# Batch 0's second feature half moved to the end of round two, in a Strassen kernel on one Trainium2 core

## Chip, core and metric

The kernel runs on one core of one Trainium2 chip. The metric is device time of one execution in microseconds (us). Before the change the median of three runs is 705.16 us (704.62 to 705.32). The core's engines are named as in the profile: PE (TensorE, matmuls), PEld (its weight loads), DVE (VectorE), ACT (ScalarE), POOL (GpSimd) and SP (SyncE, which here only issues transfers). All data in the computation are float32.

## The reference

Two blocks follow one another. The first is a cross attention between 512 tokens and 32 states, for 8 batches and 8 heads of width 64:

```python
scores = scale * np.matmul(x, state.transpose(0, 1, 3, 2))      # x (8,8,512,64), state (8,8,32,64)
a = softmax(scores)                                            # over the 32 states
xread = np.matmul(a, state)
a2 = softmax(scale * np.matmul(state, x.transpose(0, 1, 3, 2))) # over the 512 tokens
sread = np.matmul(a2, x)
attn = np.concatenate([xread, sread], axis=2)                  # 512 + 32 rows per batch
```

Its output, with the heads side by side, is a matrix of 8 x 544 = 4352 rows and 512 columns. The second block is a feed-forward layer with 2048 features:

```python
h = x @ w_in                                    # w_in (512, 2048)
g = h * erf(softplus(h))
return g @ w_out                                # w_out (2048, 512)
```

Both weights arrive as float64. The kernel reads them as pairs of 32-bit words and makes float32 from them: two ACT and three DVE instructions for each piece.

## The kernel before, in words

**Tiling.** The 2048 features fall into 16 tiles of 128, four groups of four tiles (g = 0 to 3), and two feature halves (u = 0: groups 0 and 1; u = 1: groups 2 and 3). The 4096 token rows are taken batch by batch, 512 at a time; the 256 state rows of all batches (`sread`) are taken together. For the token rows, `xread @ w_in` is not formed by way of `xread`: the states are multiplied by `w_in` first (`mixed`, L1138; `mixed_part`, L613 for batch 0), which gives "mixed weights" of 256 x 512 for a group, and these are multiplied by the transposed attention weights `aT` (the first product). Softplus, erf and the gating multiply follow, then the product with `w_out` (the second product).

**Three schemes of product.** Plain: batch 0's first product (L624, `first`) and second product (L631, `second`), 128x512 matmuls. One level of Strassen, seven products for eight: every other first product (`first_product`, L1237) and the second products of the first half for batches 1 to 5 (`second_product`, L1321). Two levels, 49 products for 64: the second products of the first half for batches 6 and 7 and of the second half for batches 1 to 7 (`twice_product`, L1508). The sums of blocks that Strassen needs are DVE instructions: `sums_a` (L1288) and `sums_y` for activations, `sums_w` (L429) for one level and `sums_b` (L1383) for two levels of `w_out`, L1490 for two levels of activations.

**Stages.** *Start*: load batch 0 and the weights; attention of batch 0; batch 0 is computed whole, all four groups, while the weights are fetched (1 MB at a time into one of three `raw` buffers, L157) and converted (L167, L169 on ACT, L172 to L174 on DVE). All 16 pieces of `w_in` and `w_out` are converted here. The second half of `w_in` is written to a DRAM scratch (`kept_in`, L745), since its place in `ring` is needed. Attention of batch 1 is fitted in. *Round one*: units u = 0 of batches 1 to 7, one after the other. A unit is the sums over its activations, the mixed weights of the next batch, the attention of the batch after that, its second product, and the next batch's first product with softplus, erf and multiply. From each batch's attention `aT` and its sums are saved to DRAM (`keep_y`). In batch 2 the second half's `w_out` and its sums are saved (`keep_w`), since batches 6 and 7 need the space. *States*: the 256 state rows for both halves (L1676, L1725). *Round two*: units u = 1 of batches 1 to 7; `bring_y` reloads the attention. Their results are added to the rows in DRAM by POOL's accumulating transfers (L1556). The last unit, batch 7, instead reloads its output rows into `ring` tiles and adds to them: each quarter result is copied or added from PSUM (ACT L1518, DVE L1523), summed into a block of 128x512, and joined (L1568); four 256 KB stores (L1572) follow.

**What sets the order.** The start follows a list written out by hand (`order0`), one name per step. From the last 40 steps of it on, each operation is declared by `op(engine, cost, at, go, reads, writes, table, land)`. `emit` takes a table `ORDER` with a fixed order for every engine, plays the operations through with their costs to get begin times, and traces them in that order; `at` is not used there. `in_order` then fixes this order on PE, DVE, ACT and SP. `adopt` hands the dependences of one set of buffer names to another.

Of the kernel before, what the change touches and what calls it, by code (L numbers as in the profile page):

```python
# [9 lines left out]
F32 = mybir.dt.float32  # L10
# [7 lines left out]
def kernel(  # L18
# [21 lines left out]
    P = 128  # L40
# [29 lines left out]
    x_t = {}  # L70


    def load_x(b):
        t = xin.tile([P, NC, H, D], F32, name="x")
        for h in range(H):
            nc.sync.dma_start(out=t[:, :, h, :], in_=x[b, h].rearrange("(c p) d -> p c d", p=P))
        x_t[b] = t
# [4 lines left out]
    def in_order(begun, engines=(nc.tensor, nc.vector, nc.scalar, nc.sync)):  # L82

        last = {}
        for i in nc.cur_bb.bb.instructions[begun:]:
            if i.engine in last:
                tc.add_manual_dep(i, last[i.engine].name, mybir.DependencyInfo(
                    mybir.DependencyClass.NoSync, mybir.DependencyReason.DATA), reason="in_order")
            if i.engine in [e.engine for e in engines]:
                last[i.engine] = i  # L90

    begun = traced()

    xq_t = {}

    def load_xq(b, hs=range(H)):
        if b not in xq_t:
            xq_t[b] = xin.tile([P, NI, S // Ns, Ns], F32, name="xq")  # L100
# [8 lines left out]

    st = const.tile([P, B, P], F32, name="st")  # L110
    away0 = ring[:, 1, 0].rearrange("p k i t -> p (k i t)")
    st0 = away0[:, 512:640].rearrange("p (g d) -> p g d", g=2)
    x0 = xin.tile([P, NC, H, D], F32, name="x").rearrange("p c h d -> p (c h d)").rearrange(
        "p (h c d) -> p h c d", h=H, c=NC)
    x_t[0] = x0.rearrange("p h c d -> p c h d")
    for i in range(NI):
        (nc.scalar, nc.sync)[i % 2].dma_start(
            out=x0[:, 2 * i:2 * i + 2].rearrange("p h c d -> p h (c d)"),
            in_=x[0, 2 * i:2 * i + 2].rearrange("h (p c) d -> p h (c d)", c=NC))
        if i == 1:  # L120
            nc.sync.dma_start(out=st0, in_=state[0].rearrange("(g h) n d -> (h n) g d", g=2))

    def load_st(hs):
        for h in hs:
            i, e = h // 2, h % 2
            nc.sync.dma_start(out=st[Ns * i:Ns * i + Ns, 1:B, D * e:D * e + D],
                              in_=state[1:B, h].rearrange("b n d -> n b d"))


    w_in = const.tile([P, NF // 2, NK, P], F32, name="w_in")  # L130
    away = ring[:, :, 2].rearrange("p u k i t -> p u (k i t)").rearrange(
        "p u (j k f) -> p u j k f", k=NK, f=P)
    of_group = [w_in[:, GF * g:GF * g + GF] for g in range(2)] + [away[:, u] for u in range(2)]
    pieces_in = [of_group[j // 2][:, 2 * (j % 2):2 * (j % 2) + 2] for j in range(NF // 2)]
    kept_in = dram.tile([P, NF // 2, NK * P], F32, name="kept_in")
    w_out = const.tile([P, NF, d_model], F32, name="w_out")

    fetched = []

    def weight(dst, src, parts=1):  # L140

        flat = lambda t: t.rearrange("p a b c -> p (a b c)" if len(t.shape) == 4 else
                                     "p a b -> p (a b)")
        if src.dtype == F32:
            fetched.append(nc.sync.dma_start(out=dst, in_=src))
            return [lambda: None] * 2 * parts, [lambda: None] * 3 * parts  # L150
        raw = act.tile([P, 2 * 2 * d_model], U32, name="raw", bufs=3)
        blocks = [(raw, src)]
        if len(src.shape) == 4:
            blocks = [(raw.rearrange("p (h x) -> p h x", h=2)[:, h], src[:, h]) for h in range(2)]
        for to, part in blocks:
            part = part.bitcast(U32)
            fetched.append(nc.sync.dma_start(  # L157
                out=to.rearrange("p (a b) -> p a b", a=part.shape[1]), in_=part))
        n, m = dst.shape[1] // parts, d_model // parts * 4
        on_act, on_dve = [], []  # L160
        for k in range(parts):
            to, words = dst[:, n * k:n * k + n], raw[:, m * k:m * k + m]
            words = words.rearrange("p (n w) -> p n w", w=2)
            lo, hi, to = words[:, :, 0], words[:, :, 1], flat(to)
            d = to.bitcast(U32)
            on_act += [
                lambda to=to, hi=hi: nc.scalar.activation(out=to, in_=hi.bitcast(F32),  # L167
                                                          func=ACTF.Copy, scale=2.0 ** -112),
                lambda lo=lo: nc.scalar.activation(out=lo, in_=lo, func=ACTF.Copy,  # L169
                                                   scale=2.0 ** -29)]  # L170
            on_dve += [
                lambda d=d: nc.vector.tensor_scalar(d, d, 3, None, op0=ALU.logical_shift_left),  # L172
                lambda on=nc.vector, d=d, lo=lo: on.tensor_tensor(d, d, lo, op=ALU.add),
                lambda d=d, hi=hi: nc.vector.scalar_tensor_tensor(  # L174
                    out=d, in0=hi, scalar=0x80000000, in1=d, op0=ALU.bitwise_and,
                    op1=ALU.bitwise_or)]
        return on_act, on_dve

    gw = GF * P

    def weights_in(j):
        return weight(pieces_in[j], moe_w_in[:, 2 * P * j:2 * P * j + 2 * P].rearrange(
            "(k p) (h f) -> p h k f", p=P, f=P), 2 if j == 0 else 1)

    def weights_out(j):
        return weight(w_out[:, 2 * j:2 * j + 2, :],
                      moe_w_out[2 * P * j:2 * P * j + 2 * P].rearrange("(t p) e -> p t e", p=P))

    leads = [0]
# [4 lines left out]

    def lead(out):

        warm(out, leads[0])
        leads[0] = 0

    sT = const.tile([P, NK, 2, Ns, B // 2], F32, name="sT")  # L200
    st00 = away0[:, 768:1024]
    where = {h: (g, q) for g, hs in enumerate(((0, 2, 1, 3), (5, 7, 4, 6)))
             for q, h in enumerate(hs)}
    aT = {}

    def all_of(jobs):
        for f in jobs:
            f()
# [7 lines left out]
    marks = []  # L216

    def scored(b, xT, pool=ps_at, names=("at", "at")):


        s2 = [pool.tile([P, S], F32, name=name) for name in names]
        for i in reversed(range(NI)):
            for e in range(2):
                r, q = slice(D * e, D * e + D), slice(Ns * i, Ns * i + Ns)
                on_pe = nc.tensor.matmul(out=s2[e][q, :], lhsT=st[r, b, q], rhs=xT[r, i, :],
                                         start=True, stop=True)
        marks.append(on_pe)
        return s2

    def scores(b, xT, *pool):  # L230
        s2 = scored(b, xT, *pool)
        on_pe = marks.pop()
        sc = att.tile([P, 2, S], F32, name="sc")
        for e in range(2):
            last = nc.scalar.copy(sc[:, e], s2[e])
        marks[:] = last, on_pe
        return sc, last

    def largest(sc):
        m2 = small.tile([P, 2], F32, name="m2")  # L240
        for e in range(2):
# [1689 lines left out]
```

## Time and profile before

The profiled execution spans 702.93 us; the median of the runs is 705.16 us.

| what | us |
|---|---|
| median of three runs | 705.16 |
| span of the profiled execution | 702.93 |
| PE busy, in the span | 694.6 |
| DVE busy | 571.8 |
| ACT busy | 469.3 |
| POOL busy | 58.9 |
| first product of batch 0 begins | 19.05 |
| first second product of batch 1 begins (L1321) | 126.46 |
| first product of two levels (L1508) begins | 345.86 |
| last matmul begins | 697.65 |

The profiler records one execution. A float32 matmul appears as two MATMUL records, whose starts are one streaming time apart; each record also holds the time that the data needs to run through the array, so successive records overlap, and prices are best taken from the distance between starts. The same holds for short DVE and ACT instructions, to a smaller extent. "Busy" is the time in which an engine has at least one record open. Stretches of one kind on one engine are merged in the timeline and in the chain ("x24" is 24 records).

### The profile page before, as it was taken

How to read it: one execution, taken by the hardware profiler on the slowest of the kernel's cores; microseconds unless marked ns; L12 is line 12 of the kernel's file. 1: busy time of each engine (PE TensorE's matmuls, PEld its weight loads, DVE VectorE, ACT ScalarE, POOL GpSimd, SP SyncE). 2: the span in 40 equal slices, each digit the busy share in tenths (PEclk: the TensorE clock that was granted, in tenths of full speed). 3: DMA queues.
4: the chain of work that ended last, by engine and by line, in shares of the span. 5: the costliest groups of instructions: out<-in, count | busy, mean ns of one | idle time of the engine just before them, and what ended most of it. 6: DMA issues, size and time to landing. Idle time of an engine off the chain costs nothing.

```text
span 702.9 us, 12986 instructions
## 1 busy us (share of the span) xinstructions
PE 694.6 (99%) x5039; PEld 565.4 (80%) x5039; DVE 571.8 (81%) x930; ACT 469.3 (67%) x812; POOL 58.9 (8%) x54
## 2 busy tenths in 40 slices
PE   8999999999999999999999999999999999999997
PEld 7444346687878778787999998798989898989997
DVE  6997887999979788696969753896979587778997
ACT  5999898949576655838473455846585756666842
POOL 0000000000000000000001000102021221212322
PEclk9999999999999999999999999999999999999999
DMA  8869582845648746352234514405152663435665
GB/s 261 260 194 252 191 192 46 201 86 108 179 85 259 198 81 201 55 173 53 93 98 120 161 58 165 98 31 96 17 98 33 111 75 69 60 42 65 104 94 106
DMA packets 159886, 85.54 MB, mean 122 GB/s; under 512 B 123728, under 2 KB 149328, under 8 KB 159056
## 3 DMA queue, kind: packets, MB, share of 16 engines
q1 hardware_dynamic: 146224, 71.59, 36.5%
q0 software_dynamic: 13056, 12.59, 14.3%
q8 instruction: 40, 0.66, 0.4%
q10 hardware_dynamic: 544, 0.52, 0.2%
q14 instruction: 22, 0.18, 0.1%
HBM read 46.27 MB, written 34.73 MB: 115 GB/s over the span
## 4 chain that ended last, share of the span: by engine, by line
PE 94%; DVE 4%; issue 0%; ACT 0%; DVEq 0%; ACTq 0%
PE o L1508 28%; PE o L1321 17%; PE h L1237 17%; PE o L631 8%; PE at L1237 7%; PE o L1725 3%; PE h L1676 3%; PE h L624 2%; PE at L624 2%; PE h L1138 2%; PE at L1138 2%; PE at L1676 1%; PE at L1100 1%; PE h L997 1%; PE at L613 1%; DVE ring L1568 1%
## 5 line engine op out<-in xcount | busy, mean ns | idle before, releaser
L1249 ACT COPY ring<-h 128x512 f32<-128x512 f32 x112 | 64.7, 586 | 84.3 <-PE h L1237 81.2
L1237 PE MATMUL h<-aT,m 128*128 128x256 f32 x336 | 85.1, 380 | 0.0
L1277 DVE TENSOR_TENSOR ring<-ring 128x1024 f32<-128x1024 f32 (+1 forms) x60 | 68.6, 1146 | 14.0 <-ACT ring L1274 13.4
L1321 PE MATMUL o<-w_out,ring 128*128 128x256 f32 x320 | 77.7, 383 | 0.0
L1321 PEld LDWEIGHTS o<-w_out,ring 128*128 128x128 f32 x320 | 59.6, 190 | 15.9 <-issue 5.9
L1259 ACT ACTIVATE ring<-ring 128x512 f32<-128x512 f32 x112 | 66.7, 631 | 6.6 <-PE o L1321 2.1
L1237 PEld LDWEIGHTS h<-aT,m 128*128 128x128 f32 x336 | 61.8, 190 | 10.4 <-ACT ring L1249 0.8
L1288 DVE TENSOR_TENSOR ring<-ring 128x1024 f32<-128x1024 f32 x56 | 67.8, 1217 | 0.3
L631 PE MATMUL o<-w_out,ring 128*128 128x512 f32 x128 | 59.7, 599 | 0.0
L1508 PE MATMUL o<-w_out,w_in 128*128 128x128 f32 x448 | 59.6, 275 | 0.0
L1274 ACT ACTIVATE ring<-ring 128x1024 f32<-128x1024 f32 (+1 forms) x60 | 59.0, 1004 | 0.2
L1321 PE MATMUL o<-raw,ring 128*128 128x256 f32 x240 | 58.9, 381 | 0.1
L1508 PE MATMUL o<-w_out,ring 128*128 128x128 f32 x432 | 58.8, 276 | 0.0
L1508 PEld LDWEIGHTS o<-w_out,ring 128*128 128x128 f32 x432 | 54.1, 192 | 4.2 <-issue 1.7
L1508 PEld LDWEIGHTS o<-w_out,w_in 128*128 128x128 f32 x448 | 56.0, 192 | 1.7 <-issue 0.8
L1556 POOL DMA_DIRECT2D out_dram<-oo x14 | 17.0, 1213 | 448.5 <-ACT o L1529 360.8
L1321 PEld LDWEIGHTS o<-raw,ring 128*128 128x128 f32 x240 | 45.3, 190 | 9.5 <-issue 2.5
L631 PEld LDWEIGHTS o<-w_out,ring 128*128 128x128 f32 x128 | 23.7, 190 | 27.6 <-issue 26.2
L1508 PE MATMUL o<-raw,ring 128*128 128x128 f32 x324 | 44.7, 276 | 0.0
L1508 PEld LDWEIGHTS o<-raw,ring 128*128 128x128 f32 x324 | 41.3, 192 | 2.4 <-issue 1.7
L1251 DVE TENSOR_TENSOR ring<-ring,at 128x512 f32<-128x512 f32 x28 | 19.1, 684 | 23.5 <-ACT ring L1249 21.8
L1508 PE MATMUL o<-raw,xT 128*128 128x128 f32 x288 | 37.3, 275 | 0.0
(289 smaller groups left out, 1391.5 us busy)
## 6 DMA issues: line engine op xcount, KB each, us to landing
raw<-in_moe_w_in_dram SPq DMA_DIRECT2D x16, 512.0 KB, 4.8
raw<-in_moe_w_out_dram SPq DMA_DIRECT2D x8, 1024.0 KB, 5.3
xq<-in_x_dram SPq DMA_DIRECT2D x112, 64.0 KB, 2.5
x<-in_x_dram SPq DMA_DIRECT2D x56, 128.0 KB, 3.2
out_dram<-oo SPq DMA_DIRECT2D x10, 512.0 KB, 3.7
kept_a<-aT SPq DMA_DIRECT2D x7, 512.0 KB, 3.2
aT<-kept_a SPq DMA_DIRECT2D x7, 512.0 KB, 4.6
out_dram<-oo POOLq DMA_DIRECT2D x14, 256.0 KB, 4.4
```

The source lines that it names most:

```text
L624: nc.tensor.matmul(out=h_t[g, i], lhsT=m_t[0, g][:, e, P * i:P * i + P], rhs=aT[0][:, e], start=start, stop=not start)
L631: nc.tensor.matmul(out=acc[r], lhsT=gT[g][:, i, P * r:P * r + P], rhs=w_out[:, GF * g + i, :], start=(made_of[r] == 1), stop=(made_of[r] = ...
L1138: nc.tensor.matmul(out=bank(names[e])[q, :], lhsT=st[r, b, q], rhs=of_group[2 * u + j][r, :, i, :], start=True, stop=True)
L1237: nc.tensor.matmul(out=out_[:, i], lhsT=x_[:, q:q + P], rhs=y_, start=(start and i == 0), stop=(i == 1), skip_group_check=not start)
L1249: op(ACT, 0.5, t, lambda: nc.scalar.copy(out_(), view(bank(name))), [name], w)
L1259: op(ACT, 0.53, t, lambda: nc.scalar.activation(out=part(splane, k), in_=part(hplane, k), func=ACTF.Softplus), area(hplane, ks=[k], os=[o] ...
L1274: op(ACT, 0.085 + 0.875 * share, at + n, lambda s_=s_: nc.scalar.activation(out=s_, in_=s_, func=ACTF.Erf), [], area(splane, ks=[k], os=os ...
L1277: op(DVE, 0.065 + 1.075 * share, at + n + 1, lambda s_=s_, h_=h_: tt(s_, s_, h_, op=ALU.mult), area(hplane, ks=[k], os=os), area(splane, k ...
L1288: op(DVE, 1.14, at + k, lambda k=k, x_=x_, y_=y_, how=how: tt(get("h", k), get(*x_), get(*y_), op=how), area(v[x_[0]], ks=[x_[1]]) + area( ...
L1321: nc.tensor.matmul(out=view(name)[:, h], lhsT=lhs[:, i, :], rhs=weight_of[n]()[:, u, i, :], start=(start and h == 0 and i == 0), stop=(h = ...
L1508: nc.tensor.matmul(out=out_[:, Q2 * k:Q2 * k + Q2], lhsT=lhs[:, k, i], rhs=rhs[:, i], start=first, stop=(k == len(ns) - 1 and i == 1), ski ...
L1676: nc.tensor.matmul(out=bank(bk)[:, P * i:P * i + P], lhsT=x_[:, i, k], rhs=y_[:, k], start=(start and i == 0 and k == 0), stop=(i == GF - ...
```

## The change

- Batch 0's groups 2 and 3 are left out of the start. Its products over groups 0 and 1 stay plain, and its rows are stored from these alone. Its attention is summed and saved like every other batch's (`sums_y(0)`, `keep_y(0)`), and batch 0 becomes the eighth and last unit of round two, in two levels of Strassen. Batch 7, which was last, is now added to DRAM by POOL like the others.
- The weights of the second half are no longer converted in the start. `stage(n)`, 16 times, fetches one tile of `w_in` or `w_out` into half of a `raw` buffer and converts it during round one; a tile of `w_in` goes from there to `kept_in` (eight saves of 256 KB in place of two of 1 MB). The sums of the second half's `w_out` and `keep_w` move from batch 2 to batch 5.
- `order0`, with `start0`, `groups0`, `weights0` and `next0`, is gone. The start is declared by `op` like the rest (`begin0`, `mixed0`, `first0`, `serf0`, `second0`, `put0`, `fetch_pair`, `convert_pair`), with the transfers as a pipe in `emit` (`pipe`, `FIXED`). `ORDER` is new for all five engines, from the first instruction on, and `in_order` now holds for POOL too. Some copies out of PSUM change engine (`BY_VECTOR` names those on DVE). The two exponentials of batch 0's token weights move ahead of the first softplus.
- In the last unit, the last of the five groups of products (`ns == (3,)`) adds its quarter results from PSUM straight into the output tile (`into`), and the last block is stored in three pieces of 128, 64 and 64 KB.

The core of the diff:

```diff
-    def in_order(begun, engines=(nc.tensor, nc.vector, nc.scalar, nc.sync)):
+    def in_order(begun, engines=(nc.tensor, nc.vector, nc.scalar, nc.sync, nc.gpsimd)):
...
-    STARTS = {PE: 0.0, ACT: 1.3, DVE: 2.5, SP: 0.0, GP: 0.0}
+    STARTS = {PE: 0.78, ACT: 0.74, DVE: 1.0, SP: 0.74, GP: 1.0}
     LAG = {PE: 0.24, ACT: 0.16, DVE: 0.17, SP: 0.2, GP: 0.2}
+    FIXED = 2.1
...
-                    free[e] = begin[n] + cost
-                    end[n] = free[e] + land
+                    end[n] = free[e] = begin[n] + cost
+                    end[n] += land
+                    if pipe:
+                        piped = max(piped, end[n]) + pipe
+                        end[n] = piped + FIXED
...
+    def second0(g, r, i, at):
+
+        def go():
+            made_of[r] += 1
+            nc.tensor.matmul(out=bank("o%d" % r), lhsT=gT[g][:, i, P * r:P * r + P],
+                             rhs=w_out[:, GF * g + i, :], start=(made_of[r] == 1),
+                             stop=(made_of[r] == NF // 2))
+
+        op(PE, 0.86, at, go, gT_of(g, i) + [("Wo", GF * g + i), "oacc%d" % r], [])
...
+            if final is not None and ns == (3,):
+                join_others()
+
+                def into(frm, h, q, t, region=region, of_bank=of_bank):
+                    to = mine(0, 1)[:, h, Q2 * q:Q2 * q + Q2]
+                    op(DVE, 0.2, t, lambda: tt(to, to, region[frm](), op=ALU.add),
+                       [of_bank[frm]], area(final, us=[0], ks=[2 + h], os=[q]))
+
+                copy = add = into
...
-            join(0, 1, R3, at + 22)
-            store(0, 1, at + 22)
...
+        if final is not None:
+            for h, qs in (1, slice(0, 2)), (0, slice(0, 1)), (0, slice(1, 2)):
+                cols = slice(Q2 * qs.start, Q2 * qs.stop)
+                op(SP, 0.4, at + 26, lambda h=h, cols=cols: nc.sync.dma_start(
+                    out=quad(0, 1)[:, h, cols], in_=mine(0, 1)[:, h, cols]),
+                   area(final, us=[0], ks=[2 + h], os=range(qs.start, qs.stop)), [], land=2.2)
...
+    for kind, j, k, at, then in (("i", 0, 0, 2.2, 8.5), ("i", 1, 1, 3.3, 13.4), ("o", 0, 2, 5.2, 16),
+                                 ("o", 1, 0, 16.2, 22), ("i", 2, 1, 22.6, 32), ("i", 3, 2, 26.3, 37),
+                                 ("o", 2, 0, 30.5, 39), ("o", 3, 1, 37.2, 43.5)):
+        fetch_pair(kind, j, k, at)
+        convert_pair(kind, j, k, then)
...
+    def stage(n, at):
+        f, k, e = NF // 2 + n // 2, n % 3, n // 2 % 2
+        if n % 2:
+            fetch_out(f, k, 1, at)
+            convert(("o", f), half(k, 1), w_out[:, f], RAW(k, [1]), [("Wo", f)], at + 5)
+        else:
+            fetch_in(f, k, 1, at)
+            convert(("i", f), half(k, 1), mt(3)[:, e], RAW(k, [1]), [("mS", 1, e)], at + 5)
+            op(SP, 0.45, at + 10, lambda: nc.sync.dma_start(
+                out=kept_in[:, f - NF // 2], in_=mt(3)[:, e]), [("mS", 1, e)],
+               [("kin", f - NF // 2)], land=3.0)
+
+    for n in range(NF):
+        stage(n, BASE + 8 + 8 * n)
...
-                          3 - hplane if u and b == B - 1 else None)
+                          3 - hplane if u and b == 0 else None)
...
-            if b == 2:
-                sums_w(1, base + 20, 1, 2, 4, 3)
-                keep_w(base + 30)
+            if b == TWICE - 1:
+                sums_w(1, base + 5, 1, 2, 4, 3)
+                keep_w(base + 12)
...
-    hq = {b: 2 if b % 2 else 1 for b in range(1, B)}
+    turns = [*range(1, B), 0]
+    hq = {b: 2 if b % 2 else 1 for b in turns}
...
-    for b in range(1, B):
...
+    for n, b in enumerate(turns):
+        nxt = turns[n + 1:n + 2]
...
-        unit(b, 1, base + 34.5 * (b - 1), 0, hq[b], follow, between)
+        unit(b, 1, base + 34.5 * n, 0, hq[b], follow, between)
 
     emit()
-    in_order(begun, [nc.tensor, nc.vector, nc.scalar])
+    in_order(begun)
```

## The prediction

> **What bounds the kernel now.** I read the page's busy shares, then the chain that ended last, then busy time by stage, then single rows for prices.
>
> The busy shares and the chain's shares by engine:
>
> ```profile
> PE 694.6 (99%) x5039; PEld 565.4 (80%) x5039; DVE 571.8 (81%) x930; ACT 469.3 (67%) x812; POOL 58.9 (8%) x54
> ...
> PE 94%; DVE 4%; issue 0%; ACT 0%; DVEq 0%; ACTq 0%
> ```
>
> TensorE is the bound from end to end: it is idle for 8.3 us in all. So a change is worth the matmul time that it removes, less the gaps that it opens. Where gaps could open is read from the stages. The cuts are: first product of batch 0 (19.05), first second-layer product of batch 1 (126.46), batch 6, where twice-Strassen begins (345.86), round two's first unit (463.0), last matmul (698.3).
>
> ```profile
> core 0: us, PE busy (x) PEld busy (x) DVE busy (x) ACT busy (x) POOL busy (x), PEclk, DMA share, GB/s
> 0.00:19.05 19.05, 16.44 (x197) 14.28 (x197) 12.35 (x27) 10.92 (x17) 0.69 (x6) 1.00 0.80 263
> 19.05:126.46 107.41, 107.41 (x565) 50.59 (x564) 91.71 (x128) 99.42 (x126) 0.00 (x0) 1.00 0.69 193
> 126.46:345.86 219.40, 218.39 (x1558) 175.54 (x1557) 189.95 (x324) 144.23 (x241) 0.00 (x0) 1.00 0.55 136
> 345.86:463.00 117.14, 117.14 (x871) 107.74 (x871) 83.38 (x137) 66.15 (x123) 7.38 (x6) 1.00 0.37 105
> 463.00:698.30 235.30, 235.24 (x1856) 217.23 (x1854) 193.10 (x317) 148.58 (x308) 50.84 (x42) 1.00 0.45 72
> 698.30:702.93 4.63, 0.00 (x0) 0.00 (x0) 1.28 (x3) 0.00 (x0) 0.00 (x0) 0.89 0.39 132
> ```
>
> In each row the first number after the stretch is its length. From 19.05 on TensorE has no gap but 1.0 us in the third stage, at full granted clock. In the second row ScalarE is busy 99.4 of 107.4 us (93%) and VectorE 91.7 (85%), in the third VectorE 190.0 of 219.4 (87%). These two are the near-bounds, and they stand exactly where the change takes TensorE work out.
>
> **Matmuls removed.** The chain of waits (start, length, engine, line, records; a float32 matmul leaves two records) and the timeline of TensorE give the prices:
>
> ```profile
> 27.78 10.30 PE o L631 x24
> 41.02 3.44 PE h L624 x8
> ...
> 109.53 1.73 PE h L1237 x8
> ...
> 658.87 29.09 PE o L1508 x260
> ```
>
> ```profile
> 58.05 0.66 PE L613 MATMUL at<-ring 64*32 64x256 f32 x16
> 58.65 1.98 PE L631 MATMUL o<-w_out,ring 128*128 128x512 f32 x4
> ...
> 446.84 1.09 PE L1138 MATMUL h<-x,st 64*32 64x512 f32 x16
> 447.73 1.06 PE L1138 MATMUL at<-xq,st 64*32 64x512 f32 x16
> 448.72 1.13 PE L1725 MATMUL o<-raw,ring 128*128 128x256 f32 x4
> ```
>
> Groups 2 and 3 of batch 0 leave the start phase: 32 plain second-layer matmuls are 64 records at 10.30/24 = 0.429, 27.5 us. The 16 first-layer matmuls are 32 records at 3.44/8 = 0.43, 13.8 us. Four blocks of mixed weights take 58.65 - 58.05 = 0.60 each, 2.4 us. Together 43.7 us, all on the path, since the second stage has no gap.
>
> **Matmuls added**: one more unit at the end of round two. Its two mixed products take 448.72 - 446.84 = 1.9 us; its first product is 56 records at 1.73/8 = 0.216, 12.1 us; its 49 small products are 196 records at 29.09/260 = 0.112, 21.9 us. Sum 35.9 us. Successive units of round two now start their mixed products at 446.85 and 624.09, five units apart, 35.4 each, which agrees. Net of both: **-7.8 us**. Warm-up and spare products are as many as before (8 and 22).
>
> **The tail.** The last block no longer goes through a quarter add and then a 128x512 join; each quarter is added from PSUM straight into the output tile.
>
> ```profile
> 697.65 0.61 PE L1508 MATMUL o<-w_out,w_in 128*128 128x128 f32 x4
> ...
> 698.61 0.28 DVE L1523 TENSOR_TENSOR sc<-sc,o 128x128 f32<-128x128 f32 x1
> 698.99 0.69 DVE L1568 TENSOR_TENSOR ring<-ring,sc 128x512 f32<-128x512 f32 x1
> ```
>
> The join starts at 698.99 and ends 0.8 after the quarter add's end (699.68 against 698.89). After it 3.25 us of store and end remain. The last store shrinks from 256 to 64 KB; landings of small stores are 2.2 us at 256 KB and 1.9 at 32 KB, so that adds nothing to 0.3. Against it, six VectorE adds replace four ScalarE copies, two VectorE adds and the join: about even for VectorE. I take **-0.7**, bounds -1.1 and 0 (the adds queued behind others).
>
> **VectorE, the price of the move.** Conversions of the second-half weights (8 MB in eight pieces) leave the start and come back as 16 half pieces in round one. Durations of one piece, groups of the second stage:
>
> ```profile
> L174 DVE SCALAR_TENSOR_TENSOR w_out<-raw,w_out 128x1024 uint32<-128x1024 uint32 x8 | 9.8, 1221 | 0.1
> L173 DVE CUSTOM_DVE_ANT_0 w_out<-raw,w_out 128x2048 uint16<-128x2048 uint16 x8 | 9.7, 1219 | 0.0
> L172 DVE TENSOR_SCALAR w_out<-w_out 128x1024 uint32<-128x1024 uint32 x8 | 5.5, 685 | 0.0
> ```
>
> Back-to-back records overlap by 0.08 us (a 0.68 us one is followed after 0.60), so a piece occupies 0.685 + 1.219 + 1.221 - 0.24 = 2.9 us, and a half piece (0.42, 0.68 and 0.68 in the first microseconds) 1.54. From 19.05 to 345.86 VectorE is busy 91.7 + 190.0 = 281.7 us; by their start times 113 of its 452 records come after a gap, so packed it needs 281.7 - 113 x 0.08 = 272.7. The change takes out eight pieces (23.1), eight gating multiplies (4.8), six copies of mixed weights (2.0) and three copies that go to ScalarE (1.4); it adds 16 half pieces (24.6) and the sums of batch 0's attention (1.4). Left: 272.7 - 31.3 + 26.0 = 267.4 us. The time for it shrinks from 326.8 to 326.8 - 43.7 = 283.1: **from 83 to 94.5%**. Nothing hides VectorE work beyond that. Its best 60 us now (130 to 190) hold 58.0 us busy, 97%, with TensorE dense in all but 0.1 us, so 94.5% can be had, but not for long without bursts that someone waits for. What is late then is a product's operand, for TensorE.
>
> **ScalarE in the start.** Of its 99.4 us the change removes 16 conversions (about 1.08 apart, 17.2), eight softplus (4.4) and eight erf (4.7), twelve table loads from 60 to 107 us (15.4), six copies (2.0) and one load for the early exponentials (1.3): 45.0. It gains about 6 (copies from VectorE 2.1, halves of the first stages 3.6, others 0.3). Left: 60.5 us in 107.4 - 43.7 = 63.7, 95% where it held 93%. At 93% the start takes 65.1, 1.4 us more.
>
> The Trainium skill, ScalarE: Activation LUTs, "What ACT_TABLE_LOAD costs", speaks against this: every switch of set costs about 2.66 us, of which 1.38 is a drain. By it some twelve loads left in the start would take 16.6 us more, and the kernel would come out near 713. In this trace a load of 1.28 us begins at 19.85 and the activation behind it at 21.15, so the measured price stands.
>
> **Waits and queues.** Fetches of the half pieces wait in SP's queue for a buffer that VectorE frees; queued behind are the reloads of x, the turned attention weights and the outputs. SP now issues some 27 us per unit of 40 and gets about 4 more, so it has room. The save of the combined weights moves from batch 2 to batch 5, and 28 sums wait for it before batch 6; its copies now land in 6.6 to 8.1 us, and a unit is long enough. Batch 7's seven POOL accumulates (1.2 us each, POOL 8% busy), the saved and reloaded attention of batch 0 and the smaller stores of w_in lie under matmuls: nothing. Until 19.05 the same loads and steps run in nearly the same order: nothing, bounds -0.5 and +1.
>
> New gaps from both engines: bounds -1.0 (today's last 1.0 us of gaps vanishes too) and +10.9 (VectorE held at 91%: 267.4/0.91 = 294.0, against 283.1). I take **+3.0**, near the low end, since the ScalarE row alone gives 1.4 and VectorE still fits.
>
> **Sum**: 702.9 - 7.8 - 0.7 + 3.0 = 697.4 us of span. The runs' median, 705.16, lies 2.2 above the profiled span, so 699.6.
>
> **Rivals.** *Everything stays packed*: the orders keep TensorE as dense as now. For it: dense now at 97% of VectorE; against: 94.5% on average. 702.9 - 7.8 - 1.1 - 0.5 + 2.2 = 695.7. *The start is bound by ScalarE*: it holds only the 86% that it had from 100 to 120 us (17.1 of 20), 60.5/0.86 = 70.3, 6.6 us over; with the net, 705.2 - 8.5 + 6.6 = 703.3. For it: its alternation of softplus and erf tables on the path; against: it held 98% from 20 to 60 us. *Slower, VectorE becomes the bound in round one*: the half pieces sit among the attention of batches 3 to 6. It decides from a density below 267.4/(283.1 + 8.5) = 91.7%; at the 91% above, 10.9 more, the time is 705.2 - 8.5 + 10.9 = 707.6. For it: averaged over 19 to 346 us it has never had to exceed 86%; against: 45 us of its idle time cost nothing today. *The change doesn't do what it says*: the added unit runs uncovered, batch 0's reloads of attention (3.3 to 4.6 us to landing) arriving late; with all of today's 7 to 8 us of net gain lost in waiting, 704 to 705.
>
> The skill's TensorE: Matmul & The Clock Gate, Part 1, warns that idling past its window of about 3.4 us halves the clock until another such window is busy; a gap that long would cost 1.7 us more, and no row here shows one.
>
> **Chances.** Forecast (697 to 702.5) 0.50; packed 0.20; ScalarE 0.12; VectorE 0.15; uncovered 0.03. No change is within 0.2%, 1.4 us (703.75 to 706.6). Faster: 0.50 + 0.20 + 0.06 of the ScalarE case = 0.76; same: the other 0.06 and the uncovered 0.03 = 0.09; slower 0.15. The range, 695.8 to 705.8, leaves out the ends of the packed and the VectorE case; the likeliest case's own is 697 to 702.5.
>
> **What would show it.** Right: the plain second-layer product with 64 records where it had 128, the small products with 196 more, all at the spacings above; the first second-layer product of batch 1 near 84 us; VectorE at 93% or more up to batch 6; last matmul to end about 3.9 us. Wrong: TensorE gaps above 6 us in sum between 19 us and batch 6 (then one of the two engine rivals, told apart by which engine the gaps wait for), or a unit of round two far from 35.4 us.

## The result, and the profile after

The changed kernel takes **727.11 us** (median of four runs, 725.36 to 728.30) against 704.89 for the kernel before in the same session: ratio 1.0314, 95% interval 1.0297 to 1.0331, slower. Its profiled execution spans 723.3 us. The prediction, 699.6 us and faster, was wrong.

The page's busy shares and the chain's shares by engine, after (instructions as x, then shares of the span):

```profile
PE 699.6 (97%) x5163; PEld 581.9 (80%) x5163; DVE 592.3 (82%) x988; ACT 472.7 (65%) x850; POOL 67.8 (9%) x61
...
PE 67%; DVE 14%; DMA 9%; SPq 5%; ACT 3%; issue 2%; DVEq 0%; POOL 0%; ACTq 0%; POOLq 0%
```

TensorE is still busy 97%, but only two thirds of the chain that ended last are now its own. Transfers (DMA) and SP's issuing (SPq), absent from the chain before, hold 14%, VectorE another 14%.

Busy time by stage, after. The cuts are the first product of batch 0, the first second-layer product of batch 1, the first product of two levels, and the last matmul record:

```profile
core 0: us, PE busy (x) PEld busy (x) DVE busy (x) ACT busy (x) POOL busy (x), PEclk, DMA share, GB/s
0.00:20.98 20.98, 17.42 (x197) 14.92 (x197) 12.80 (x27) 13.47 (x22) 0.69 (x6) 0.97 0.91 281
20.98:87.75 66.77, 63.50 (x394) 30.47 (x394) 62.19 (x98) 57.59 (x83) 0.00 (x0) 0.98 0.69 174
87.75:317.58 229.83, 217.78 (x1457) 169.91 (x1451) 204.59 (x353) 159.75 (x266) 0.00 (x0) 0.99 0.64 161
317.58:718.49 400.91, 400.64 (x3126) 366.56 (x3124) 311.91 (x511) 241.87 (x481) 67.12 (x55) 1.00 0.43 85
718.49:723.33 4.84, 0.27 (x3) 0.08 (x1) 0.84 (x3) 0.00 (x0) 0.00 (x0) 0.96 0.50 163
```

In round one (third row) TensorE is idle for 12.0 of 229.8 us, where 1.0 of 219.4 had been idle. Yet VectorE is busy only 204.6 of these, 89%, and ScalarE 70%: no engine is full there.

How much time was lost is worked out record by record: each matmul record is given the distance to the next record's start that its kind has in dense stretches of the kernel before, and what a distance has beyond that is "lost" (gaps, and records stretched by a lower clock). The last three columns are kernels of the experiments below; "stage transfers out" is e1, "new orders" is e9, "SP's alone" e12; the figures are those of the profiled executions.

| lost, us | before | after | stage transfers out | SP's alone | new orders |
|---|---|---|---|---|---|
| to batch 0's first product | 4.3 | 6.2 | 7.8 | 6.6 | 5.8 |
| to batch 1's second layer | 5.3 | 10.1 | 10.9 | 7.5 | 6.3 |
| to the first product of two levels | 9.9 | 27.2 | 14.6 | 16.8 | 8.7 |
| to the last matmul | 5.7 | 9.6 | 9.6 | 9.3 | 7.3 |
| sum | 25.2 | 53.1 | 42.9 | 40.2 | 28.1 |
| sum of the dense distances | 672.1 | 664.7 | 664.7 | 664.7 | 664.7 |

(The stage cut at 345.86 in the record of the prediction lies 6.9 us behind the first product of two levels before, which is at 339.01; the table uses 339.01.) So the change took 7.4 us of matmul time out and lost 27.9 us: 702.9 - 7.4 + 27.9, less 0.1 in the tail, is the 723.3 of the span. Of the 27.9, 17.3 arose in round one.

**What the largest gap waits for.** Waits by engine and line, after, from 87.75 to 317.58 us (us in total, times, longest):

```profile
ACT m L539 <- DMA kept_in<-m: 6.7, 1, 6.7
...
DVE w_out L543 <- ACT w_out L539: 5.1, 1, 5.1
...
PE o L1000 <- ACT o L1025: 4.6, 1, 4.6
ACT m L539 <- DMA raw<-in_moe_w_in_dram: 4.6, 2, 2.3
ACT oo L1010 <- DMA out_dram<-oo: 4.3, 1, 4.3
```

L539 is the first conversion instruction of a staged half piece; L1010 copies a result into `oo`. In the timelines of SP, ScalarE and TensorE around 155 us (start, length, engine, line; in brackets the idle time before and who ended it) one sees how that becomes TensorE's largest gap:

```profile
136.38 10.75 SPq L751 DMA_DIRECT2D sc<-xT  x16
147.23 0.54 SPq L1020 DMA_DIRECT2D out_dram<-oo  x1
147.81 0.47 SPq L861 DMA_DIRECT2D kept_a<-aT  x1
148.32 0.84 SPq L862 DMA_DIRECT2D kept_y<-sy  x1
149.27 1.14 SPq L531 DMA_DIRECT2D raw<-in_moe_w_out_dram  x1
150.45 1.42 SPq L1020 DMA_DIRECT2D out_dram<-oo  x1
151.91 1.04 SPq L1526 DMA_DIRECT2D kept_in<-m  x1
```

```profile
158.21 0.66 ACT L539 ACTIVATE m<-raw 128x512 f32<-128x512 f32 x1 [6.66 <-DMA kept_in<-m]
158.78 0.57 ACT L928 COPY ring<-h 128x512 f32<-128x512 f32 x1
159.25 0.59 ACT L1025 COPY o<-o 128x512 f32<-128x512 f32 x1
```

```profile
159.89 2.07 PE L1000 MATMUL o<-w_out,ring 128*128 128x256 f32 x4 [4.64 <-ACT o L1025]
161.75 3.45 PE L1000 MATMUL o<-raw,ring 128*128 128x256 f32 x12
```

SP is in a burst of 16 issues from 136.4 to 147.1, and five transfers stand ahead of the save (L1526) of a converted half tile. It is issued at 151.9 and lands at 158.2, 6.2 us later. The next half piece goes into the same half tile, so ScalarE waits 6.66 us at L539. The copy out of PSUM that TensorE needs, L1025, had to come third behind it in ScalarE's written order.

### The profile page after: what moved, and what is told of

It reads as the page before. It is cut to its first block, busy times and chain, and to the rows that moved or that the text cites. A ratio compares the mean times of both kernels' runs of the same rounds, so it can differ in the third digit from the quotient of the medians.

```text
span 723.3 us, 13325 instructions
## 1 busy us (share of the span) xinstructions
PE 699.6 (97%) x5163; PEld 581.9 (80%) x5163; DVE 592.3 (82%) x988; ACT 472.7 (65%) x850; POOL 67.8 (9%) x61
## 4 chain that ended last, share of the span: by engine, by line
PE 67%; DVE 14%; DMA 9%; SPq 5%; ACT 3%; issue 2%; DVEq 0%; POOL 0%; ACTq 0%; POOLq 0%
PE o L1236 25%; PE h L916 15%; PE o L1000 10%; PE at L916 6%; PE o L1419 3%; SPq L93 3%; PE h L1370 2%; DMA raw<-in_moe_w_out_dram 2%; DMA x<-in_x_dram 2%; DMA raw<-in_moe_w_in_dram 2%; PE at L817 1%; PE h L817 1%; DMA aT<-kept_a 1%; DVE xq L673 1%; PE at L1370 1%
## 5 line engine op out<-in xcount | busy, mean ns | idle before, releaser
L916 PE MATMUL h<-aT,m 128*128 128x256 f32 x360 | 91.8, 381 | 1.6 <-ACT sc L686 1.4
L1000 PEld LDWEIGHTS o<-w_out,ring 128*128 128x128 f32 x320 | 59.9, 191 | 23.4 <-ACT o L1025 5.0
L938 ACT ACTIVATE ring<-ring 128x512 f32<-128x512 f32 x120 | 72.0, 633 | 7.8 <-DVE ring L934 4.3
L1236 PE MATMUL o<-w_out,w_in 128*128 128x128 f32 x512 | 69.5, 277 | 0.0
L1236 PEld LDWEIGHTS o<-w_out,w_in 128*128 128x128 f32 x512 | 64.6, 192 | 5.9 <-issue 2.5
L1236 PE MATMUL o<-w_out,ring 128*128 128x128 f32 x480 | 64.9, 277 | 0.0
L1236 PEld LDWEIGHTS o<-w_out,ring 128*128 128x128 f32 x480 | 60.0, 192 | 3.9 <-ACT oo L1246 1.7
L1156 POOL DMA_DIRECT2D out_dram<-oo x16 | 24.0, 1589 | 398.4 <-DMA out_dram<-oo 345.6
L1236 PEld LDWEIGHTS o<-raw,xT 128*128 128x128 f32 x320 | 39.3, 192 | 0.6
L916 PE MATMUL at<-aT,sx 128*128 128x256 f32 x120 | 31.2, 383 | 0.4 <-DVE ring L930 0.3
L916 PE MATMUL h<-sy,m 128*128 128x256 f32 x120 | 31.1, 382 | 0.0
```

Of the source, the lines that this page charges most:

```text
L916: nc.tensor.matmul(out=out_[:, i], lhsT=x_[:, q:q + P], rhs=y_, start=(start and i == 0), stop=(i == 1), skip_group_check=not start)
L938: op(ACT, 0.53, t, lambda: nc.scalar.activation(out=part(splane, k), in_=part(hplane, k), func=ACTF.Softplus), area(hplane, ks=[k], os=[o] ...
L1000: nc.tensor.matmul(out=view(name)[:, h], lhsT=lhs[:, i, :], rhs=weight_of[n]()[:, u, i, :], start=(start and h == 0 and i == 0), stop=(h = ...
L1156: op(GP, 1.2, t, lambda: nc.gpsimd.dma_start(out=quad(r, c), in_=one(v), accum_op=ALU.add), every(*v), [("out", b, r, c)], land=6.0)
L1236: nc.tensor.matmul(out=out_[:, Q2 * k:Q2 * k + Q2], lhsT=lhs[:, k, i], rhs=rhs[:, i], start=first, stop=(k == len(ns) - 1 and i == 1), ski ...
```

## The experiments

The **theory**: the new orders were made for transfers that end earlier than they do. In-order engines stand before words or buffers that a transfer has not freed yet, with the copies that TensorE needs behind them. **Rival A**: VectorE and ScalarE are full (the prediction's own rivals). **Rival B**: the start, or the clock, is the loss. **Rival C**: the transfers' volume as such. All ratios are to the kernel before (704.8 to 705.1 us in these sessions). e1 to e4, e6 to e8 and e11 are medians of two runs; those of e1 lie 4.4 us apart, of e2 7.3, of e3 and e8 3.0 to 3.2.

| run | median us | ratio, 95% interval |
|---|---|---|
| e1, stage transfers out | 712.81 | 1.011 (1.0036 to 1.0183) |
| e2, stage conversions out | 722.64 | 1.0249 (1.0127 to 1.0372) |
| e3, both out | 713.02 | 1.0113 (1.0061 to 1.0164) |
| e4, stage transfers on GpSimd's queue | 722.39 | 1.0246 (1.0216 to 1.0275) |
| e5, orders anew | 716.57 | 1.0163 (1.0138 to 1.0189) |
| e6, second maximum later | 726.66 | 1.0309 (1.0289 to 1.033) |
| e7, block weights not saved | 723.66 | 1.0267 (1.0246 to 1.0287) |
| e8, seven saves out | 721.27 | 1.0233 (1.0204 to 1.0261) |
| e9, orders anew, with slack | 700.69 | 0.9937 (0.9913 to 0.9961) |
| e10, the same from another start | 701.52 | 0.9949 (0.9934 to 0.9964) |
| e11, spare products | 727.76 | 1.0323 (1.0302 to 1.0343) |
| e12, SP's order alone | 712.47 | 1.0111 (1.0094 to 1.0128) |
| e13, the engines' orders alone | 708.20 | 1.0052 (1.0035 to 1.007) |

### Transfers or conversions: e1, e2, e3

```diff
@@ e1
-            fetch_out(f, k, 1, at)
+            op(SP, 0.45, at, lambda: None, [], RAW(k, [1]), pipe=1.8)
...
-            op(SP, 0.45, at + 10, lambda: nc.sync.dma_start(
+            op(SP, 0.45, at + 10, lambda: f > NF // 2 or nc.sync.dma_start(
...
@@ e2 (convert, for the staged pieces alone)
-        op(ACT, 1.05 if full else 0.57, at, lambda: nc.scalar.activation(
+        op(ACT, 1.05 if full else 0.57, at, lambda: skip or nc.scalar.activation(
```

e1: 

> Leaves out the stage's transfers (the 16 fetches and 7 of the 8 saves of the second-half weights; round two reads the one saved row eight times); the conversions stay, on stale words, as does every engine's order. Against 727.1 us of the changed kernel. Theory (late transfers hold the engines' fixed orders: the stage's conversions stand in ScalarE's and VectorE's queues ahead of the copies that TensorE waits for): the TensorE gap of 4.6 us at 155 us goes, of the 16.5 us lost in round one some 10 to 15 come back, 712 to 717 us. Rival A (the engines are full: the conversions' own 72 instructions are what is too much): at most 3 us come back, 724 to 727. Rival B (the start and the clock alone): 726 to 727.

e2: 

> Leaves out the 80 conversion instructions of the stage on ScalarE and VectorE; its fetches and saves stay where they are, and w_out's second half is set to zero by GpSimd at the start. Theory (late transfers): with nothing on an engine that waits for a fetch, the engines are no more held by the stage, though SP's queue is as full as before: 712 to 718 us, about as the run without the transfers. Rival A (engines full): 711 to 715, and well below the run without the transfers. Rival B: 726 to 727.

e3: 

> Leaves out both, transfers and conversions of the stage. This is what the stage costs in all. Theory: 710 to 715, within 3 us of the run without the transfers. Rival A (engines full): as the run without the conversions, and 8 or more below the run without the transfers. Rival B (the loss is not the stage's): 724 to 727.

(The conversions are 16 times five, 80 instructions, also where the first text says 72.) Without the transfers 14.3 us come back, and leaving out the conversions as well brings nothing more that can be seen: 712.8 and 713.0. So the conversions' own time is not what is lost, and rival A falls. Without the conversions but with the transfers only 4.5 us come back (its two runs: 719.0 and 726.3). That was below what I expected: the transfers also hurt without anyone converting. The timelines of e2 (its lines from L107 on stand one higher), SP, ScalarE and TensorE, show one way:

```profile
242.86 9.14 SPq L766 DMA_DIRECT2D x<-in_x_dram  x8
...
253.95 1.67 SPq L1021 DMA_DIRECT2D out_dram<-oo  x2
```

```profile
261.19 0.58 ACT L1011 COPY oo<-o 128x512 f32<-128x512 f32 x1 [9.33 <-DMA out_dram<-oo]
```

```profile
262.83 1.95 PE L818 MATMUL h<-w_in,st 64*32 64x512 f32 x14 [6.80 <-ACT ring L929]
```

The eight issues of x, 5.0 us in the plan, take 9.1 here. The outputs behind them in SP's queue start late, `oo` is not free, ScalarE stands 9.3 us and TensorE 6.8. So it need not be a transfer of the stage that comes late: here it is x and an output.

### Which transfers: e4, e7, e8

e4 issues the stage's transfers from GpSimd (`nc.gpsimd` for `nc.sync` in the three places); e8 has only the second of e1's edits; e7:

```diff
-        op(SP, 2.4, at, lambda: [nc.sync.dma_start(out=k, in_=t) for t, k in weights_of(1)],
+        op(SP, 2.4, at, lambda: None,
...
-        op(SP, 2.4, at, lambda: [nc.sync.dma_start(out=t, in_=k) for t, k in weights_of(1)],
+        op(SP, 2.4, at, lambda: None,
```

e4: 

> Issues the stage's 16 fetches and 8 saves from GpSimd's queue in place of SP's, everything else as in the changed kernel, output complete. Theory, with SP's in-order queue (bursts of 16 issues, about 11 us) as what makes the transfers late: they start when their buffer is free, the gap at 155 us goes, 714 to 720 us. Rival (the DMA engines, not the queue, make them late): 725 to 728. Rival A (engines full): 725 to 728.

e7: 

> Leaves out the saving of the second half's block weights (3.5 MB) and their fetching back, so that round two's second layer reads other blocks. Theory (late transfers): an output and x that stand behind the save in SP's queue no more land late at 247 to 262 us, the TensorE gap of 2.1 us there and what follows goes, 721 to 724. Rival B (start alone) and A: 726.5 to 727.5.

e8: 

> Leaves out seven of the eight saves of the first layer's second half (256 KB each; round two reads the one saved row eight times); fetches and conversions stay. At 151 us ScalarE waits 6.7 us for such a save before it may write the half tile anew, and TensorE 4.6 us behind it. Theory: the gap at 155 us goes, and 4 to 7 us with it, 720 to 723. If the fetches are what is late, 725 to 727.

e7 gives back 3.5 us and e8 5.8, both as expected. e4 gives 4.7, less than expected: off SP's queue the fetches land later instead (6.2 and 8.6 us after their issue, in the chain that ended last). So neither one transfer nor SP's queue as such is the whole cause; each of these gives back its own few us.

### The start and the clock: e6, e11

```diff
@@ e6 (ORDER, DVE)
-            0-1 12 76 13 2-3 14-16 39 17 4 7-8 77-78 5-6 9-11 41 40 18-21 82 22-24 42 25-26 44-45 43
+            0-1 12 13 2-3 14-16 39 17 4 7-8 5-6 9-11 76-78 41 40 18-21 82 22-24 42 25-26 44-45 43
@@ e11
-            spare_products("o%d" % g, 3 if g else 14, 12.6 + 5 * g)
+            spare_products("o%d" % g, 12 if g else 23, 12.6 + 5 * g)
```

e6: 

> Only VectorE's order in the first 20 us: the three instructions of batch 0's second maximum (L475, L477: 0.55, 0.60 and 0.17 us), which nothing needs before 35 us, go behind the normalisation (L465) that the first products wait for. Theory of the start (VectorE is the chain there, and the idle TensorE's clock then falls to half for 3.4 us): first product of batch 0 0.8 to 1.3 us earlier, 724 to 726.5 in place of 727.1. Rival (the start's loss is the transfers' or ScalarE's): 727.

e11: 

> The changed kernel with nine more spare 128-column products (0.11 us each) before each of batch 0's two turnings of its weights, in which TensorE stood idle 1.1 us (at 17.1 and 18.9 us); these products' results are not read. If the half clock at 20 to 23.4 us follows from TensorE's idleness before it, the clock stays at 1.00 there and the first products end 1.5 us earlier; 725 to 727 us in all, since VectorE's conversions come next. Rival (the half clock has another cause): it is there again, and the time is 727 or more.

(The first text's L475, L477 and L465 are L474, L476 and L464.) e6 brought batch 0's first product from 20.98 to 20.70 us, a third or less of what was expected, and the time (726.66) cannot be told from 727.11. In e11 the eighteen products took more than the idle time and put the first product back to 23.96. Its clock did stay at 1.00 from 18 to 24 us, but the time did not fall: 727.76. Not every execution has the half clock there: it is absent from those profiled of e6, e7 and e8 too, and the orders of the last two are the changed kernel's (why it comes and goes is in the last section). Of rival B there are the 1.9 us of the table's first row. e11 traded the half clock for a start 3.0 us later; e6's profiled execution has no half clock there, starts 0.3 us earlier, and still takes 727.11 us. So rival B is not where the time went; the 4.8 us of the second row fall to 1.0 with e9's orders.

### The orders: e5, e9, e10, e12, e13

Only the text of `ORDER` differs from the changed kernel, and in it not GpSimd's part: every instruction and every transfer is there. A search moved single operations within an engine's order, played the kernel's list of operations through with a price for each, and kept the move if the end came earlier. For e5 the prices of transfers were taken roughly from the trace. For e9 and e10 they came from the landings of every SP transfer in two traces, with up to 30% and 2.5 us of delay on each transfer to spare, and with one more price that the first plan does not have: 0.12 us between two instructions of one engine of which the second needs the first's result. e12 moved SP's entries alone, e13 those of the three engines alone. SP's order begins, for e9:

```diff
-            0-1 5 2 6 9 7-8 17 10 3-4 12 11 19-20 18 23 13 24 14 21-22 15-16 40 37 25 39 32 29 27 26
+            0-1 5 2 6 9 7-8 3 10 4 23 17 24 18 11-12 14 13 15 20 19 22 21 16 40 37 39 25
```

e5: 

> Nothing left out: the changed kernel's instructions and transfers, all of them, each on its engine and queue; only the five written orders are made anew, by working the list of operations through with what the trace shows of transfers (16 issues of x or of the turned weights in 10 to 11 us of SP, 512 KB landing 4.5 to 6.2 us after issue, one after the other) in place of the plan's own 2 to 4 us. Theory (the orders were made for transfers that end earlier than they do, so that in-order engines stand before late words): most of the 28 us lost goes, 695 to 706 us. Rival C (the transfers as such are too much for the DMA engines or for SP in this window): 715 or more whatever the order. Rival A (engines full): 715 or more.

e9: 

> Nothing left out; the orders made anew once more, now with the landings that the two traces show transfer by transfer (one server: 2.0 to 2.2 us for a 512 KB fetch, 6.5 for x turned, 4.5 for x, 8.5 for the block weights' save, 1.7 us behind each; SP held while the server is behind), 0.12 us between instructions of one engine that follow from each other, and with up to 30% and 2.5 us of delay on each transfer to spare. Theory (orders made for transfers that end too early; the first new orders still had no slack): 694 to 708 us, below the first new orders' 716.6. Rival C (the transfers' volume, not the orders): 713 to 720, as the first new orders.

e10: 

> The same as the run before it, made from another starting order: 694 to 708 by the theory, within 4 us of it; 713 to 720 by rival C.

e12: 

> Nothing left out; only SP's order of its 123 entries is made anew (same measured landings, same slack as in the 700.7 us kernel), the orders of TensorE, ScalarE and VectorE are those of the changed kernel. If the lateness arises in SP's queue (fetches and outputs behind bursts of 16 issues), this alone gives back over half of the 26 us: 707 to 713. If it arises where the engines' orders put the words' use too early, it gives back less than a third: 719 to 725.

e13: 

> The reverse: the orders of TensorE, ScalarE and VectorE anew, SP's as in the changed kernel. If the lateness arises in SP's queue: less than a third comes back, 719 to 725. If in the engines' orders, which use the words too early and have what TensorE needs behind them: over half, 705 to 713.

e5 fell short of its range: 10.5 us came back, not 21 or more. By what was written down before, its 716.6 spoke for rivals A and C (715 or more); e9 and e10 are what refutes them. They came out within their ranges, 700.7 and 701.5 us: **25.0 of the 27.9 us lost are gone (26.4 in the medians) with nothing left out, and e9 is faster than both kernels**, than the one before by 0.6% (0.4 to 0.9). Rival C falls with that: the same 89 MB are moved. Whether the better prices of transfers, the slack or the 0.12 us made the difference from e5 was not separated. Busy time by stage of e9 (its lines stand 19 higher than the changed kernel's):

```profile
20.59:81.83 61.24, 59.64 (x328) 29.03 (x329) 58.25 (x93) 56.17 (x82) 0.00 (x0) 1.00 0.68 171
81.83:300.89 219.06, 219.06 (x1545) 175.20 (x1544) 208.74 (x361) 167.44 (x273) 0.00 (x0) 1.00 0.69 178
300.89:693.48 392.59, 392.59 (x3097) 361.23 (x3096) 307.50 (x507) 238.19 (x477) 67.35 (x55) 1.00 0.43 84
```

In round one TensorE is dense while VectorE is busy 208.7 of 219.1 us, 95%. In e9's list of waits from 81.83 to 300.89 us the longest for a transfer that is left reads:

```profile
PEld at L798 <- DMA xq<-in_x_dram: 0.8, 1, 0.8
```

No conversion waits for a fetch or a save there. e12 and e13 each give back over half, 14.6 and 18.9 us, together more than the 26.4 of e9. They are not the two halves of e9: each was searched for anew, with the other side's orders left as they were. So the question which order is at fault has no single answer: starting the transfers earlier and using their words later are two ways to get back much of the same time.

## Why the prediction was wrong

**Matmuls, -7.8: right.** The dense distances fell by 7.4 us. The pieces are there: the plain second-layer products have half their records, and the products of two levels 196 more (1764 to 1960). The unit of round two, predicted at 35.4 us, is 36.3 (644.35 - 462.65 for five).

**Tail, -0.7: too large.** From the start of the last matmul record to the end 4.94 us became 4.84, 0.1 less where 0.7 was forecast; the quarter adds go straight into the tile, but three stores are issued one after another behind them.

**VectorE and ScalarE, the two near-bounds: right in themselves.** 267.4 us of VectorE work were to fit into 283.1 us, 94.5%; in e9 it is 58.25 + 208.74 = 267.0 in 280.3, 95.3%, with 1.6 us of TensorE idleness (counted to the first product of two levels, 6.9 us short of the prediction's cut). Both engine rivals are refuted by that, and by e3, which removes the conversions and gains nothing over e1. The prediction's test for them, TensorE gaps above 6 us and "which engine the gaps wait for", would have misled: the largest gap does wait for ScalarE, but for a copy that stands behind a wait for a transfer. Batch 1's second layer began at 87.75, not near 84; in e9 it begins at 81.83.

**"Waits and queues": the step that failed.** It says that SP "has room" and puts the stage's transfers at nothing, with bounds for the new gaps (-1.0 to +10.9) taken from the engines' density alone; "until 19.05" was put at nothing as well. The term +3.0 came out at +27.9: 1.9 until the first product, 4.8 in the start, 17.3 in round one, 3.9 after it. What the runs show in its place: 14.3 us come back with the stage's transfers left out (e1), 14.6 with a new order of SP's transfers alone (e12), and 26.4 with new orders for all four engines (e9). With the orders of e9 it is 28.1 - 25.2 = +2.9, and the whole is 700.7 where 699.6 was predicted. So the sum described what the change can do with orders that fit; it said nothing of the orders that it has. That +2.9 and +3.0 agree so closely is in part luck: the +3.0 was picked between bounds 12 us apart, and e10, made in the same way as e9, is 0.8 us slower. The "27 us per unit of 40" for SP is an average, too: by the trace before, SP's issues add up to 37.0 us between 127 and 168 us and to 19.9 between 289 and 330.

**What the orders were made for, and what came.** The diff carries the transfer times that the orders were made for: a fetch of a `w_in` tile is 0.45 to issue, 1.42 in the pipe and `FIXED = 2.1`, some 4.0 us; of a `w_out` tile 4.35; a save 0.45 and `land=3.0`, 3.45. The page before has, from issue to landing:

```profile
raw<-in_moe_w_in_dram SPq DMA_DIRECT2D x16, 512.0 KB, 4.8
raw<-in_moe_w_out_dram SPq DMA_DIRECT2D x8, 1024.0 KB, 5.3
```

and the page after, with the medians of the same names:

```profile
raw<-in_moe_w_in_dram SPq DMA_DIRECT2D x16, 512.0 KB, 4.9
...
raw<-in_moe_w_out_dram SPq DMA_DIRECT2D x8, 512.0 KB, 6.2
```

The medians before do not give the error away: the first row's fetches come in pairs, which the plan has at 4.0 and 4.9 us, and a fetch of 1 MB is 6.05 in it. What the plan lacks is the spread. The stage's 16 fetches take 3.6 to 7.8 us, and of its eight saves the view of L1526, after, says (issue time in ns, lowest, median and highest, then the same of the landing):

```profile
L1526 SPq DMA_DIRECT2D kept_in<-m x8: 437/861/1631, 94.9 to 255.1; - x8
...
DMA to landing us min/median/max: 3.2/5.3/9.4
```

In e9 the same saves take 2.3 to 5.0 us. With its own prices the changed kernel's plan has the last matmul at 685.7 us; it came at 718.5. The plan has little room for the error: SP issues in it for 176 of the 214 us from 41 to 255 us. It does queue the fetches behind one another: the four of 512 KB that SP issues between 1.75 and 5.04 us land 5.6, 6.7, 9.0 and 11.2 us after their issue, and 5.4, 6.6, 10.6 and 11.6 in the plan. But x, the turned weights, the outputs and the saves, in the same queue, have a fixed time each. The Trainium skill, DMA: Bandwidth & Descriptors, "Anatomy of one DMA", has a price per transfer, measured on GpSimd's path: about 2.0 us fixed, and the size over 436 GB/s. By it, as an estimate, 512 KB would take 3.2 us; no fetch here was that quick.

The plan's prices of TensorE, VectorE and ScalarE agree with the trace (a 128x512 add 0.60 from start to start, in both), with one exception. An instruction that needs the result of the one just before it on its engine begins at once in the plan, and later in the trace (VectorE, after):

```profile
14.31 0.68 DVE L461 TENSOR_REDUCE z1b<-ring 128x16 f32<-128x512 f32 x1
14.91 0.68 DVE L454 TENSOR_REDUCE m1b<-at 128x16 f32<-128x512 f32 x1
15.62 0.69 DVE L456 TENSOR_TENSOR ring<-at,m1b 128x512 f32<-128x512 f32 x1
```

L454 does not read what L461 writes and starts 0.60 after it; L456 reads L454's maxima and starts 0.71 after it. So part of the loss may come from this wait and not from transfers. No run tested that alone, and e9's orders take both into account. How much it may weigh is estimated by playing the loop of `emit` through once more, with the orders of the two kernels and other prices (the last matmul's start, us):

| prices | the changed kernel's orders | e9's orders |
|---|---|---|
| the plan's own | 685.7 | 686.0 |
| 0.12 us more behind such an instruction on VectorE and ScalarE | 695.2 | 686.8 |
| 2 us more on each transfer | 705.8 | 695.1 |
| both | 712.2 | 696.2 |
| measured | 718.5 | 693.5 |

The 2 us are an example, not a measurement. By the plan's own prices e9's orders are no better, so e9's gain is not that of a longer search: they are better where things come later than planned. Late transfers are shown by e1 and e12, in which the orders of TensorE, VectorE and ScalarE are the changed kernel's: 14.3 and 14.6 us. How the rest of e9's 26.4 us divides between transfers and the 0.12 us stays open.

**Open.** Whether the kernel before would gain as much from orders made in the same way was not tried, so the 4.4 us between it and e9 are not all the change's for certain. Of the 28.1 us that e9 still loses, nothing was taken apart.

## What to carry to other kernels

An order that is written out is only as good as the durations it was made with. Before you predict what a replanned kernel does, compare the plan's prices with the profile, the transfers' first, and by the spread and not the median alone. Then play the plan through with everything a little later: 2 us on each transfer moved this one by 20 us, and e9's by 9. Ask what a transfer that is 3 us late holds up on an in-order engine. When you make such an order, price transfers as a queue that they share, and leave them slack.

A density of 95% on the second engine need not cost anything; a single wait of 6.7 us in an engine that is 70% busy did.

## What the runs showed of the hardware

**The half clock comes from windows that are only partly idle.** Granted TensorE clock (the figure behind the count; ahead of the count stands TensorE's busy time), after, in stretches of 3.41 us laid from the change of the clock at 19.80 us:

```profile
12.97:16.39 3.42, 3.42 (x39) 1.00 0.88 187
16.39:19.80 3.41, 1.40 (x24) 1.00 1.04 352
19.80:23.21 3.41, 3.14 (x7) 0.50 0.35 59
36.87:40.28 3.41, 2.05 (x16) 1.00 1.15 193
156.33:159.75 3.42, 0.00 (x0) 1.00 0.97 271
159.75:163.16 3.41, 3.27 (x8) 0.50 0.66 107
```

TensorE was busy 1.40 of 3.41 us, with no gap longer than 1.2, and the clock was half for the next 3.41 us, some 1.7 us of loss. The empty window in the gap at 155 us did the same; one with 2.05 us busy did not. Windows were laid in this way in every trace here, each from its own changes of clock, up to the last matmul. Of those at full clock, all 15 with at most 41% busy were followed by the half clock, four of the ten with 43 to 52%, and none with more. Of those at half clock, an empty one (e2) and those with 45, 59 and 73% busy (e6, e10, e11) were followed by a second, those with 81% and more by the full clock. So in these traces it takes more work in a window to get the clock back than to keep it. Where the windows lie differs from one execution to the next: one begins at 16.39 us here, at 15.08 in e7 and 15.30 in e8, whose start is the same and which keep the full clock there. The Trainium skill, TensorE: Matmul & The Clock Gate, Part 1, has the window's length (3413 ns, free-running) and an idle window as the cause; the length agrees, but the window need not be idle throughout. The prediction looked for a single gap of that length.

**Issuing takes longer when much is in flight.** One issue of the turned x (L93) takes 0.49 us on SP in the median, and 2.12 us at 157.79, with two outputs, two saves and two fetches issued just before; the eight issues of x take from 5.1 to 9.5 us. SP's room in a unit is therefore not found by adding up the issue times of a quieter stretch.
